# Three-term matmuls on one core: the output products of rounds two to four as seven block products

## The chip, the cores and the metric

The kernel runs on one core of a Trainium2 chip. The core has a matrix engine (PE in the profile, with its weight loads shown apart as PEld), a vector engine (DVE), a scalar engine (ACT), a general engine (POOL) and a queue engine (SP) that issues most transfers. The metric is device time in microseconds for one execution; the median of several runs counts.

## The reference

Attention with a sigmoid in place of the softmax, then a gated MLP with a spatial mixing over the sequence. Eight batches, 12 heads of 64, 448 tokens, model width 768, 1024 hidden columns of which one half (u) is gated by the other (v). All inputs are float32.

```python
scores = scale * (q @ k.T) - log(S)          # per batch and head, S = 448
x = sigmoid(scores) @ v                      # (B, S, 768)
h = relu(x @ w_in)                           # w_in 768 x 1024
u, v = h[..., :512], h[..., 512:]
v_n = (v - mean(v)) / sqrt(var(v) + 1e-6)
v_s = einsum('ts,bsd->btd', w_spatial, v_n) + b_spatial
out = (u * v_s) @ w_out                      # w_out 512 x 768
```

## The kernel before

**Rounds.** The eight batches go in four rounds of two (`m` = 0 to 3 in the code, rounds one to four in the text). A round has these stages, which PE runs one after the other: attention (scores `psc`, sigmoid on ACT, value products `pav`), the v half of the hidden layer (`pv`, with its normalisation), the spatial products (`pg`), the u half (`pu` in round one, `ua` and `ub` in the others), and the output products `po`.

**Three terms.** A float32 factor is kept as a high part and a low part, and a product is three matmuls: high by high, low by high, high by low (`TERMS`). So each operand that is made on the chip costs a rounding copy (its high part, `high` or a CAST, mostly on ACT) and a subtraction (its low part, on DVE).

**Output.** `output(b, es)` makes two of the six 128-wide pieces of one batch's output: for each piece 4 parts of the hidden dimension by 3 terms, 12 matmuls of 448 columns. Six pieces and two batches make 144 matmuls a round. One ACT copy takes two pieces to SBUF and one transfer of 448 KB stores them. The last call of the kernel drains each piece by itself.

**The u half in seven products.** In rounds two to four, `gated_by_blocks` already makes a 2 by 2 block product with seven block products instead of eight (the sums of x's blocks come from `x_sums`, those of the weight's blocks from `weight_sums`, which were made once, in round one's output and at the start of round two, and written to the DRAM tile `w7_u`). The seven blocks of 768 KB are loaded again in each round, four ahead and three while the products run. The results are collected in PSUM and in three SBUF tiles r1, r2, r3 by ACT copies and DVE adds, and `settle` multiplies them into the gates and splits the result for the output products.

**What sets the order.** `in_program_order` keeps every engine's instructions in the order in which the code writes them. An engine takes its instructions strictly in that order, so one that waits holds all behind it on its engine. `jobs` is a list of generators, and `spare(n)` writes their next n steps at the place where it stands: that is how side work for DVE and ACT is woven into a stage. Transfers are issued on SP's queue in written order, those for the next round by `start_loads` and `ahead`.

**PSUM.** `banks(name)` hands out one of four PSUM tiles of two banks each, in turn. A matmul that writes such a tile waits for the instructions that read it before.

Of the kernel before, what the change touches and what calls it, by code (L numbers as in the profile page):

```python
# [14 lines left out]
P = 128  # L15
# [20 lines left out]
def attn_gmlp_kernel(  # L36
# [58 lines left out]
    w_out_s = const.tile([P, NFC * DM // 512, 2, 512], F32R, name="w_out_s")  # L95
# [56 lines left out]
    def weight_steps():  # L152
# [26 lines left out]
        def parts(n):  # L179
            dst, i = steps[n][2:]  # L180
            if dst is None:
                return tuple(w_u[0][:, a, i * F : (i + 1) * F] for a in range(2))
            return dst[:, i, 0], dst[:, i, 1]
# [23 lines left out]

        def begin(n):
# [8 lines left out]
        def middle(n, l, low, a):  # L217
            join(l, low, a)
            nc.scalar.copy(parts(n)[0], l.bitcast(F32))
            return l.bitcast(F32)  # L220
# [197 lines left out]
    def half_of(w, o, k, n):  # L418

        block, col = divmod((o // 2 * n + k) * 2 + o % 2, 4)  # L420
        return w[:, block, :, col * P : (col + 1) * P]
# [20 lines left out]
    def block(pos):  # L442
        flat = w_u[0].rearrange("p a c -> p (a c)")
        at = pos % SLOTS_U * 2 * BLOCK
        return flat[:, at : at + 2 * BLOCK].rearrange("p (a c) -> p a c", a=2)

    def load_block(pos):
        nc.sync.dma_start(block(pos).bitcast(F32), w7_u[pos])

    def weight_sums():  # L450
# [3 lines left out]
        names = ("11", "12", "21", "22")  # L454

        def plain(name, a):
            at = names.index(name) * BLOCK
            return w_u[0][:, a, at : at + BLOCK].bitcast(F32)

# [11 lines left out]
        for i, name in enumerate(names):  # L471
            if name in ORDER:
                at = i * BLOCK
                nc.sync.dma_start(w7_u[ORDER.index(name)], w_u[0][:, :, at : at + BLOCK].bitcast(F32))
        nc.vector.tensor_add(t0, plain("21", 0), plain("21", 1))
        yield True
        nc.vector.tensor_add(t1, plain("22", 0), plain("22", 1))
# [4 lines left out]
        nc.vector.tensor_sub(t0, plain("11", 0), t0)  # L482
        yield True
        nc.vector.tensor_add(t0, t0, plain("11", 1))
# [5 lines left out]
        nc.vector.tensor_sub(t1, t1, plain("11", 0))  # L490
        yield True
        nc.vector.tensor_sub(t1, t1, plain("11", 1))
# [8 lines left out]
        nc.vector.tensor_sub(t1, plain("12", 0), t1)  # L501
        yield True
        nc.vector.tensor_add(t1, t1, plain("12", 1))
# [245 lines left out]
    def settle(b, fcs, g, pu):  # L749

        for at, by in pu if isinstance(pu, list) else [(g, pu)]:
            nc.vector.scalar_tensor_tensor(at, by, 0.0, at, op0=ALU.max, op1=ALU.mult)
        if b % 2:
            gs = [slots["tile"][:, fcs[0] + a, :, :S] for a in range(2)]
        elif b > 1 and not fcs[0]:
            gs = [slots["tile"][:, 4 + a, :, :S] for a in range(2)]
# [7 lines left out]

    def gated_by_blocks(m):

        b0, b1 = 2 * m, 2 * m + 1
        x = {
            name: [
                x_s[:, :, k * KH + ks, j * S : (j + 1) * S] for ks in range(KH)  # L770
# [3 lines left out]
        x |= {name: sums[name] for name in ("t2", "t3", "t4")}  # L774
        r1, r2, r3 = sums.pop("r")

        def products(ps, pos, mv, begins, then=None):
            w = block(pos)
            ops = [(a, ks, c) for ks in range(KH) for a, c in TERMS]
            for i in range(2):  # L780
                for n, (a, ks, c) in enumerate(ops):
                    col = (ks * 2 + i) * P
                    nc.tensor.matmul(  # L783
                        ps[i],
                        w[:, a, col : col + P],
                        x[mv][ks][:, c],
# [410 lines left out]
```

## Time and profile before

| | us |
|---|---|
| Median of 3 runs | 652.48 (651.89 to 652.49) |
| The profiled execution, its own time | 652.91 |
| Its span, first to last instruction | 651.1 |
| PE busy in the span | 646.2 (99%) |
| DVE busy | 399.3 (61%) |
| ACT busy | 311.4 (48%) |
| One round's output products (round two) | 28.80 |
| One round's block products of the u half (round two) | 25.21 |

The profile's chain is followed back from the last instruction: each piece of it ended last before the next could start. Where PE holds nearly all of that chain, a microsecond saved on PE shortens the kernel and one saved elsewhere does not, until another engine makes PE wait. Starts in the rows are microseconds from the start of the span.

### The profile page before, as it was taken

How to read it: one execution, taken by the hardware profiler on the slowest of the kernel's cores; microseconds unless marked ns; L12 is line 12 of the kernel's file. 1: busy time of each engine (PE TensorE's matmuls, PEld its weight loads, DVE VectorE, ACT ScalarE, POOL GpSimd, SP SyncE). 2: the span in 40 equal slices, each digit the busy share in tenths (PEclk: the TensorE clock that was granted, in tenths of full speed). 3: DMA queues.
4: the chain of work that ended last, by engine and by line, in shares of the span. 5: the costliest groups of instructions: out<-in, count | busy, mean ns of one | idle time of the engine just before them, and what ended most of it. 6: DMA issues, size and time to landing. Idle time of an engine off the chain costs nothing.

```text
span 651.1 us, 10058 instructions
## 1 busy us (share of the span) xinstructions
PE 646.2 (99%) x4208; PEld 501.1 (77%) x4208; DVE 399.3 (61%) x561; ACT 311.4 (48%) x377; POOL 28.3 (4%) x63
## 2 busy tenths in 40 slices
PE   9999999999999999999999999999999999999997
PEld 3645789999855678999976558899996665889997
DVE  4989789949555486836155638773516763777320
ACT  5987322323677736222277764522218774541221
POOL 0000010000000001000000001200000000220000
PEclk9999999999999999999999999999999999999999
DMA  8755113465773000047655100004944510001213
GB/s 298 253 185 184 39 59 97 144 219 209 291 292 104 27 1 1 1 145 261 218 172 172 58 2 1 2 5 143 334 172 145 172 58 1 2 1 54 92 57 113
DMA packets 25117, 77.85 MB, mean 120 GB/s; under 512 B 2416, under 2 KB 8944, under 8 KB 25072
## 3 DMA queue, kind: packets, MB, share of 16 engines
q1 hardware_dynamic: 24784, 76.98, 34.1%
q8 instruction: 33, 0.54, 0.3%
q10 hardware_dynamic: 288, 0.23, 0.1%
q14 instruction: 12, 0.10, 0.1%
HBM read 60.69 MB, written 16.52 MB: 119 GB/s over the span
## 4 chain that ended last, share of the span: by engine, by line
PE 99%; ACT 0%; DVE 0%; issue 0%
PE po L407 18%; PE pv L407 18%; PE pav L938 15%; PE psc L325 14%; PE pg L707 10%; PE ua L783 7%; PE pav L374 5%; PE ub L783 5%; PE pu L407 4%; PE psc L307 3%; PE pg L682 1%; PE warm L416 0%; ACT osb L846 0%; DVE ats L412 0%; DVE bias_s L104 0%
## 5 line engine op out<-in xcount | busy, mean ns | idle before, releaser
L407 PE MATMUL pv<-w_g_s,x_s 128*128 128x512 f32 x504 | 115.4, 390 | 0.0
L407 PEld LDWEIGHTS pv<-w_g_s,x_s 128*128 128x128 f32 x504 | 94.3, 188 | 22.3 <-issue 2.1
L289 ACT ACTIVATE ats<-psc,bias_s 128x896 f32<-128x896 f32 x102 | 95.3, 1007 | 20.3 <-PE pav L938 13.6
L325 PEld LDWEIGHTS psc<-qks 64*128 64x128 f32 x840 | 78.1, 185 | 15.2 <-issue 4.9
L325 PE MATMUL psc<-qks 64*128 64x448 f32 x840 | 89.2, 366 | 0.0
L407 PE MATMUL po<-mlp,w_out_s 128*128 128x448 f32 x396 | 82.8, 362 | 0.0
L407 PEld LDWEIGHTS po<-mlp,w_out_s 128*128 128x128 f32 x396 | 74.2, 187 | 5.0
L938 PE MATMUL pav<-ats,v 64*64 64x448 f32 x720 | 76.0, 539 | 0.0
L707 PE MATMUL pg<-w_sp_s,mlp 128*128 128x448 f32 x320 | 65.8, 363 | 0.0
L707 PEld LDWEIGHTS pg<-w_sp_s,mlp 128*128 128x128 f32 x320 | 59.7, 187 | 5.4 <-issue 1.2
L938 PEld LDWEIGHTS pav<-ats,v 64*64 64x64 f32 x720 | 28.3, 132 | 37.4 <-issue 26.6
L851 ACT COPY osb<-po 128x896 f32<-128x896 f32 x23 | 20.9, 908 | 65.2 <-PE po L407 62.0
L123 DVE TENSOR_TENSOR x_s<-pav,x_s 128x896 fp32r<-128x896 f32 x16 | 17.4, 1091 | 50.9 <-ACT x_s L122 50.9
L275 DVE TENSOR_TENSOR qks<-raw,qks 128x848 fp32r<-128x848 f32 x46 | 47.4, 1039 | 1.0
L407 PE MATMUL po<-gs,w_out_s 128*128 128x448 f32 x180 | 39.3, 362 | 0.0
L407 PEld LDWEIGHTS po<-gs,w_out_s 128*128 128x128 f32 x180 | 33.7, 187 | 2.3
L268 DVE CAST qks<-raw 128x848 fp32r<-128x848 f32 x38 | 22.7, 597 | 19.5 <-PE po L407 13.1
L653 DVE SCALAR_TENSOR_TENSOR mlp<-rv,rstd,mlp 128x512 fp32r<-128x512 f32 (+1 forms) x32 | 23.5, 750 | 17.4 <-ACT mlp L648 16.9
L783 PE MATMUL ub<-x_s,w_u_s 128*128 128x448 f32 x162 | 33.9, 362 | 0.0
L938 PE MATMUL pav<-at,v 64*64 64x448 f32 x216 | 31.9, 536 | 0.0
L783 PEld LDWEIGHTS ub<-x_s,w_u_s 128*128 128x128 f32 x162 | 30.4, 187 | 2.0
L910 DVE COPY wval_s<-psc 128x896 f32<-128x896 f32 x9 | 9.8, 1091 | 35.8 <-PE psc L325 35.8
(121 smaller groups left out, 794.1 us busy)
## 6 DMA issues: line engine op xcount, KB each, us to landing
raw<-qk_dram SPq DMA_DIRECT2D x47, 456.0 KB, 5.4
w_u_s<-w_u SPq DMA_DIRECT2D x21, 768.0 KB, 6.0
v<-v_dram SPq DMA_DIRECT2D x24, 448.0 KB, 3.4
out_dram<-osb SPq DMA_DIRECT2D x23, 448.0 KB, 2.6
wraw<-w_in_dram SPq DMA_DIRECT2D x12, 512.0 KB, 4.8
wraw<-w_out_dram SPq DMA_DIRECT2D x6, 512.0 KB, 3.8
w_u<-x_s SPq DMA_DIRECT2D x4, 768.0 KB, 3.6
w_u<-w_u_s SPq DMA_DIRECT2D x3, 768.0 KB, 5.6
```

The source lines that it names most:

```text
L268: (nc.vector.tensor_copy if b > 1 or halfway else nc.scalar.copy)(s[:, 0], raw)
L275: nc.vector.tensor_sub(s[:, 1], loaded[b, hp][:, HALF:], s[:, 0].bitcast(F32))
L289: nc.scalar.activation(at, src, AF.Sigmoid, bias=bias_s, scale=QK)
L307: nc.tensor.matmul(psc[odd * HALF : (odd + 1) * HALF, j, :S], raw[rows, :HALF], raw[rows, HALF + Q :], start=True, stop=True,)
L325: nc.tensor.matmul(psc[:, j, :S], st[rows, k : k + P], mv[rows, Q:PART], start=i == 0, stop=i == len(ops) - 1,)
L374: nc.tensor.matmul(pav[heads, odd, :S], vt[rows, t, heads], at[rows, j], start=start, stop=t == NFULL,)
L407: nc.tensor.matmul(ps, st, mv, start=i == 0, stop=i == len(ops) - 1)
L653: nc.vector.scalar_tensor_tensor(lo, rv[rows, i], rstd[rows, i : i + 1], hi.bitcast(F32), op0=ALU.mult, op1=ALU.subtract,)
L707: nc.tensor.matmul(pg[:, i, :S], st, mv, start=n == 0 and not ended, stop=n == len(ops) - 1 and ended,)
L783: nc.tensor.matmul(ps[i], w[:, a, col : col + P], x[mv][ks][:, c], start=begins and n == 0, stop=n == len(ops) - 1, skip_group_check=True,)
L851: nc.scalar.copy(osb, po[:, :, :S])
L938: ins = nc.tensor.matmul(pavs[pair][heads, i % 2, :S], vt[rows, t if t == NFULL else t + i % 2 * (NFULL + 1), heads], at[rows, j], start=i ...
```

## The change

In rounds two to four the output of two batches is made as a 2 by 2 block product too. With the blocks of the hidden activations g11, g21 (batch one, low and high half of the hidden columns) and g12, g22 (batch two), sums t1 to t4 of them are made, and `output_by_blocks` runs seven block products of 3 pieces by 2 parts by 3 terms, 18 matmuls of 448 columns each: 126 matmuls a round instead of 144. `by_blocks` is the loop that both the u half and the output now use, with one list of products (`PRODUCTS`: which moving block, and which of the accumulators X, W, Y it goes to). For the output, X is the first bank and W and Y are the second bank of three PSUM tiles `o_m_0` to `o_m_2`. `then(pos, i)` is called behind each piece i of product number pos and writes the copies, adds and stores.

The order of the products in the u half changes: the gates are now multiplied in as r1, r3, the X accumulator and r2 come, and the sums of the gated blocks are made there (`high`, `low`). Five steps that are left (`rest`) are woven into the first two products of the output by `spare(1)`.

The seven blocks of w_out: w_out_s is laid out by blocks, three plain blocks are stored at the start of round two, and the sums are made in round two's attention by `output_weight_sums` (14 yields), woven in by `spare`: one step in the first group of two head pairs, five in the second, eight in the third. At the start of `pv` in rounds two to four, four blocks for u and four for the output are loaded (768 KB each), the other three of each while the products run. The transfers for the next attention that stood ahead of the output are in part moved into it, and its first splits too (`between`, behind the product t3). The output leaves as stores of 224 KB.

```diff
-    w_out_s = const.tile([P, NFC * DM // 512, 2, 512], F32R, name="w_out_s")
+    w_out_s = const.tile([P, 2, NFC * DM], F32R, name="w_out_s")
...
+    def half_of(e, fc):
+
+        at = (((e % 2 * 2 + fc // 2) * NCC // 2 + e // 2) * 2 + fc % 2) * P
+        return w_out_s[:, :, at : at + P]
...
-    ORDER = ("11", "12", "s2", "s1", "s3", "22", "s4")
-    SLOTS_U = 4
-    w7_u = dram.tile([NB, P, 2, BLOCK], F32, name="w7_u")
+    ORDER = ("11", "12", "s2", "s3", "s1", "s4", "22")
+    NAMES = ("11", "12", "21", "22")
+    HELD = 4
...
+    def block(flat, pos):
+        at = pos % HELD * 2 * BLOCK
+        return flat()[:, at : at + 2 * BLOCK].rearrange("p (a c) -> p a c", a=2)
+
+    def load_block(flat, pos):
+        w7 = w7_u if flat is flat_u else w7_out
+        nc.sync.dma_start(block(flat, pos).bitcast(F32), w7[pos])
...
+    def keep_plain(w7, w):
+        for name in NAMES:
+            if name in ORDER:
+                at = NAMES.index(name) * BLOCK
+                nc.sync.dma_start(w7[ORDER.index(name)], w[:, :, at : at + BLOCK].bitcast(F32))
+
+    def output_weight_sums(stage):
...
+        def add(i, a, b, op=ALU.add):
+            nc.vector.tensor_tensor(low(i), a, b, op=op)
...
+        def finish(i, name):
+            nc.vector.tensor_sub(low(i).bitcast(F32R), low(i), high(i).bitcast(F32))
+            nc.sync.dma_start(w7_out[ORDER.index(name)], stage[:, i])
+
+        add(0, part("21", 0), part("21", 1))
+        yield True
+        add(0, low(0), part("22", 0))
+        yield True
+        add(0, low(0), part("22", 1))
+        nc.scalar.copy(high(0), low(0))
+        yield True
+        add(1, low(0), part("11", 0), ALU.subtract)
+        yield True
+        add(1, low(1), part("11", 1), ALU.subtract)
+        nc.scalar.copy(high(1), low(1))
+        yield True
+        finish(0, "s1")
+        yield True
...
+        finish(2, "s3")
+        yield True
+        finish(3, "s4")
+        yield True
...
+    PRODUCTS = (("11", X), ("21", W), ("t2", X), ("t3", Y), ("t1", X), ("22", X), ("t4", Y))
+    def by_blocks(flat, stationary, moving, nk, ps, then):
+
+        started = set()
+        for pos, (mv, to) in enumerate(PRODUCTS):
+            w = block(flat, pos)
+            ops = [(a, k, c) for k in range(nk) for a, c in TERMS]
+            for i, out_ps in enumerate(ps[to]):
+                for n, (a, k, c) in enumerate(ops):
+                    nc.tensor.matmul(
+                        out_ps,
+                        stationary(w, i, k)[:, a],
+                        moving[mv][k][c],
+                        start=(to, i) not in started and n == 0,
+                        stop=n == len(ops) - 1,
+                        skip_group_check=True,
+                    )
+                started.add((to, i))
+                then(pos, i)
+            if pos + HELD < NB:
+                load_block(flat, pos + HELD)
...
+        flat = slots["tile"].rearrange("p n a s -> p (n a s)")
+
+        def in_big(n):
+            at = n * 4 * S
+            t = flat[:, at : at + 4 * S].rearrange("p (a i s) -> p a i s", a=2, i=2)
...
+        homes = {
+            "11": in_big(0), "22": in_big(1), "t1": in_big(2), "t2": in_big(3),
+            "21": in_x(0), "t3": in_x(1), "t4": in_x(2),
+        }
+        hid.update({name: [[h[a][:, k] for a in range(2)] for k in range(2)] for name, h in homes.items()})
...
+        def gate(g, by, i=slice(0, 2)):
+            nc.vector.scalar_tensor_tensor(g[:, i], by, 0.0, g[:, i], op0=ALU.max, op1=ALU.mult)
+
+        def high(name, src, i=slice(0, 2)):
+            nc.scalar.copy(homes[name][0][:, i], src[:, i])
+
+        def low(name, src, i=slice(0, 2)):
+            hi, lo = homes[name]
+            nc.vector.tensor_sub(lo[:, i], src[:, i], hi[:, i].bitcast(F32))
+        def rest():
+            low("t2", g22)
+            yield True
+            nc.vector.tensor_sub(g21, g21, g22)
+            high("t4", g21)
+            yield True
+            low("t3", g12)
+            yield True
+            low("t1", g11)
+            yield True
+            low("t4", g21)
+            yield True
+
+        def then(pos, i):
+            if mv == "11":
+                nc.scalar.copy(r1[:, i], px[i])
+            elif mv == "21":
+                nc.vector.tensor_add(r1[:, i], pw[i], r1[:, i])
+                if i:
+                    gate(g11, r1)
+                    high("11", g11)
+                    low("11", g11)
+            elif mv == "t2":
+                nc.scalar.copy(r2[:, i], px[i])
+            elif mv == "t1":
+                nc.scalar.copy(r3[:, i], px[i])
+                nc.vector.tensor_add(r3[:, i], py[i], r3[:, i])
+                if i:
+                    gate(g22, r3)
+                    high("22", g22)
+                    low("22", g22)
+            elif mv == "22":
+                gate(g12, px[i], i)
+                if i:
+                    nc.vector.tensor_sub(g11, g12, g11)
+                    high("t1", g11)
+                    nc.vector.tensor_sub(g12, g22, g12)
+                    high("t3", g12)
+            elif mv == "t4":
+                nc.vector.tensor_add(r2[:, i], py[i], r2[:, i])
+                gate(g21, r2[:, i], i)
+                high("21", g21, i)
+                if not i:
+                    nc.vector.tensor_sub(g22, g22, g11)
+                    high("t2", g22)
+                else:
+                    low("21", g21, 0)
+                    low("21", g21, 1)
+
+        by_blocks(
+            flat_u,
+            lambda w, i, k: w[:, :, (k * 2 + i) * P : (k * 2 + i + 1) * P],
+            x,
+            KH,
+            {X: px, W: pw, Y: py},
+            then,
+        )
+        jobs.append(rest())
...
+    def output_by_blocks(m, final, between):
+
+        b0, b1 = 2 * m, 2 * m + 1
+        n = NCC // 2
+        tiles = [banks(f"o_{m}_{i}") for i in range(n)]
+        px, py = ([ps[:, a, :S] for ps in tiles] for a in range(2))
+        spare_u = sums.pop("r")[2]
...
+        r1 = [spare_u[:, 0], spare_u[:, 1], in_wval(2)]
...
+            else:
+                nc.sync.dma_start(out[b, e], src)
+        def then(pos, i):
+            mv = PRODUCTS[pos][0]
+            if mv == "11":
+                spare(1)
+                nc.scalar.copy(r1[i], px[i])
+            elif mv == "21":
+                if not i:
+                    spare(1)
+                nc.vector.tensor_add(r1[i], py[i], r1[i])
+                leave(b0, i, 0, r1[i])
+                spare(1)
+                if i == n - 1:
+                    spare(99)
+                    pieces("r3", 0)
+                    pieces("c12", 1)
+                    pieces("r2", 2)
+            elif mv == "t2":
+                nc.scalar.copy(later["r2"][i], px[i])
+            elif mv == "t3":
+                if i == n - 1:
+                    between()
+            elif mv == "t1":
+                r3 = later["r3"][i]
+                nc.scalar.copy(r3, px[i])
+                nc.vector.tensor_add(r3, py[i], r3)
+                leave(b1, i, 1, r3)
+            elif mv == "22":
+                nc.scalar.copy(later["c12"][i], px[i])
+                leave(b1, i, 0, later["c12"][i])
+            elif mv == "t4":
+                r2 = later["r2"][i]
+                nc.vector.tensor_add(r2, py[i], r2)
+                leave(b0, i, 1, r2)
...
+        if m < 2:
+            ahead(value_loads, n)
         ahead(attention_loads, n + 2)
+        if m < 2:
+            more_loads(m)
+
+    def more_loads(m):
+        n = m * 2 * NHP
+        if m > 1:
+            ahead(value_loads, n)
         ahead(attention_loads, n + 3)
         if m:
             ahead(value_loads, n + 2)
...
+                spare(8 if n + 4 == end else 3 if n > first else 0)
                 value_steps(1, two[2:3])
                 if n + 4 == end:
                     leave(1, value_steps(1, two[3:]))
                 value_steps(0, [(NFULL, NFULL)])
                 split_values(pavs[0], *units[n])
+                if n + 4 < end:
+                    spare(2 if n > first else 1)
...
+        if m == 1:
+            stage = const.tile([P, 4, 2, BLOCK], F32, tag="w_u", name="stage")
+            keep_plain(w7_out, w_out_s)
+            jobs.append(output_weight_sums(stage))
         attention(m)
         slots_of_mlp(m)
...
+            spare(99)
+            if m == 1:
+                w_u.append(const.tile([P, 2, NCC * F], F32R, tag="w_u", name="w_u_7"))
+            for flat in (flat_u, flat_out):
+                for pos in range(HELD):
+                    load_block(flat, pos)
...
+        def next_splits():
+            if more:
+                for n in range(3):
+                    attention_splits(*units[(m + 1) * 2 * NHP + n])
+
         if m:
             biased(b1, pairs[1])
             spare(99)
             gated_by_blocks(m)
             start_loads(m + 1)
...
-            jobs.append(weight_sums())
+
+            def between():
+                more_loads(m + 1)
+                next_splits()
+
+            output_by_blocks(m, not more, between)
+            continue
```

On PE in round two, the first instructions of the output products. In the kernel before (o_ and po_ are PSUM tiles, mlp, gs and x_s hold the gated activations), the fifth and later matmuls wait for two more split results:

```order
L407 MATMUL po_2_0_2584<-mlp_1_2053,w_out_s_67 128x448 [waits DVE_49]
L407 MATMUL po_2_0_2584<-mlp_1_2053,w_out_s_67 128x448 x5
L407 MATMUL po_2_0_2584<-gs_2_2_2541,w_out_s_67 128x448 [waits Activation_49]
L407 MATMUL po_2_0_2584<-gs_2_2_2541,w_out_s_67 128x448
L407 MATMUL po_2_0_2584<-gs_2_2_2541,w_out_s_67 128x448 [waits DVE_49]
L407 MATMUL po_2_0_2584<-gs_2_2_2541,w_out_s_67 128x448 x3
L407 MATMUL po_2_0_2584<-mlp_1_2053,w_out_s_67 128x448 x6
```

On PE in the changed kernel, round two's output from its second block product (moving x_s, g21) to the start of the third (moving mlp, t2):

```order
L845 MATMUL o_1_0_2611<-x_s_70,w_out_s_67 128x448 [waits DMAHW5_49,Activation_49]
L845 MATMUL o_1_0_2611<-x_s_70,w_out_s_67 128x448
L845 MATMUL o_1_0_2611<-x_s_70,w_out_s_67 128x448 [waits DVE_49]
L845 MATMUL o_1_0_2611<-x_s_70,w_out_s_67 128x448 x2
L845 MATMUL o_1_0_2611<-x_s_70,w_out_s_67 128x448 [waits DVE_49]
L845 MATMUL o_1_1_2612<-x_s_70,w_out_s_67 128x448 [waits Activation_49]
L845 MATMUL o_1_1_2612<-x_s_70,w_out_s_67 128x448 x5
L845 MATMUL o_1_2_2613<-x_s_70,w_out_s_67 128x448 [waits Activation_49]
L845 MATMUL o_1_2_2613<-x_s_70,w_out_s_67 128x448 x5
L845 MATMUL o_1_0_2611<-mlp_1_2076,w_out_s_67 128x448 [waits DMAHW6_49,DVE_49]
L845 MATMUL o_1_0_2611<-mlp_1_2076,w_out_s_67 128x448 x5
L845 MATMUL o_1_1_2612<-mlp_1_2076,w_out_s_67 128x448 [waits DVE_49]
```

Each piece of the second product now starts with a wait for ACT, and the pieces of the third with a wait for DVE.

On ACT in the same place, the end of round two's block products and the start of its output. Before:

```order
L122 CAST mlp_1_2053<-wval_s_74 128x2x448 [waits DVE_49]
L122 CAST gs_2_2_2541<-g_2_2_2354 128x896 [waits DVE_49]
L122 CAST mlp_1_2053<-g_3_0_2380 128x2x448 [waits DVE_49]
L851 COPY osb_2_0_2583<-po_2_0_2584 128x2x448 [waits PE_49,Activation_49]
L851 COPY osb_2_2_2611<-po_2_2_2612 128x2x448 [waits PE_49,Activation_49]
```

After (wval_s holds g22, g_2_0 g11, g_3_0 g12, g_2_2 g21, and ur and wval_s the r1 pieces of the output):

```order
L901 CAST mlp_1_2076<-wval_s_74 128x896 [waits DVE_49]
L901 CAST mlp_1_2076<-g_2_0_2356 128x896 [waits DVE_49]
L901 CAST x_s_70<-g_3_0_2412 128x2x448 [waits DVE_49]
L901 CAST x_s_70<-g_2_2_2386 128x448 [waits DVE_49]
L901 CAST mlp_1_2076<-wval_s_74 128x896 [waits DVE_49]
L901 CAST x_s_70<-g_2_2_2386 128x448 [waits DVE_49]
L998 COPY ur_1_2_2362<-o_1_0_2611 128x448 [waits PE_49]
L901 CAST x_s_70<-g_2_2_2386 128x2x448 [waits DVE_49]
L998 COPY ur_1_2_2362<-o_1_1_2612 128x448 [waits PE_49]
L998 COPY wval_s_74<-o_1_2_2613 128x448 [waits PE_49]
```

Between the drains of the first and the second output piece there now stands the rounding copy of t4 (x_s<-g_2_2, 128x2x448), which waits for DVE.

On ACT in round two's attention, the second group. Before:

```order
L122 CAST x_s_70<-pav_16_0_1795 128x2x448 [waits DMAHW3_49,DMAHW1_49,PE_49]
L289 ACTIVATE at_3_2_3_1853<-psc_3_2_3_1854,bias_s_75 128x2x448 [waits PE_49]
L1023 COPY ats_1_1459<-pav_16_1_1796 128x896 [waits PE_49,Activation_49]
L289 ACTIVATE at_3_4_3_1876<-psc_3_4_3_1877,bias_s_75 128x2x448 [waits PE_49,Activation_49]
L289 ACTIVATE ats_1_1459<-psc_3_2_1_1891,bias_s_75 128x896 [waits PE_49]
```

After:

```order
L503 CAST stage_1456<-stage_1456 128x768 [waits DMAHW3_49,DMAHW1_49,DVE_49]
L122 CAST x_s_70<-pav_16_0_1797 128x2x448 [waits DMAHW3_49,DMAHW1_49,PE_49]
L508 CAST stage_1456<-stage_1456 128x768 [waits DVE_49]
L300 ACTIVATE at_3_2_3_1863<-psc_3_2_3_1864,bias_s_75 128x2x448 [waits PE_49]
L1235 COPY ats_1_1460<-pav_16_1_1798 128x896 [waits PE_49,Activation_49]
L300 ACTIVATE at_3_4_3_1886<-psc_3_4_3_1887,bias_s_75 128x2x448 [waits PE_49,Activation_49]
```

The two rounding copies of w_out's sums (L503, L508) stand ahead of the copy of `pav` and of the short sigmoid, and wait for DVE.

## Rows read from the trace of the kernel before

**Rows 1.** The page: granted clock in 40 slices, and the chain that ended last

```profile
PEclk9999999999999999999999999999999999999999
...
PE 99%; ACT 0%; DVE 0%; issue 0%
```

**Rows 2.** The chain in order of time: start us, us, engine, tile, line, count

```profile
1.23 2.74 PE warm L416 x6
3.97 3.59 PE psc L325 x16
...
229.24 28.80 PE pv L407 x126
...
275.27 3.60 PE ua L783 x18
...
300.48 28.80 PE po L407 x144
```

**Rows 3.** Windows of round two's block products and output, engines' busy us

```profile
core 0: us, PE busy (x) PEld busy (x) DVE busy (x) ACT busy (x) POOL busy (x), PEclk, DMA share, GB/s
300.48:329.28 28.80, 28.80 (x148) 26.72 (x151) 8.42 (x11) 5.49 (x6) 0.00 (x0) 1.00 0.66 240
275.27:300.48 25.21, 25.21 (x128) 23.63 (x127) 11.91 (x16) 6.39 (x10) 0.00 (x0) 1.00 0.43 147
```

**Rows 4.** ACT's timeline in round two's block products: start us, us, [idle before <-releaser]

```profile
286.11 0.53 ACT L797 COPY ur<-ua 128x448 f32<-128x448 f32 x1 [0.37 <-PE ua L783]
...
295.66 0.94 ACT L122 CAST mlp<-wval_s 128x896 fp32r<-128x896 f32 x1 [1.82 <-DVE wval_s L752]
```

**Rows 5.** DVE's timeline in round two's block products, last part

```profile
293.88 0.62 DVE L800 TENSOR_TENSOR ur<-ub,ur 128x448 f32<-128x448 f32 x1 [1.18 <-ACT ur L797]
294.54 1.09 DVE L752 SCALAR_TENSOR_TENSOR wval_s<-ur,wval_s 128x896 f32<-128x896 f32 x1
296.64 1.09 DVE L123 TENSOR_TENSOR mlp<-wval_s,mlp 128x896 fp32r<-128x896 f32 x1 [1.01 <-ACT mlp L122]
297.64 1.15 DVE L752 SCALAR_TENSOR_TENSOR g<-ua,g 128x448 f32<-128x448 f32 x2
```

**Rows 6.** The page's costliest groups: the output's weight loads, the attention's splits; busy, mean ns

```profile
L407 PEld LDWEIGHTS po<-mlp,w_out_s 128*128 128x128 f32 x396 | 74.2, 187 | 5.0
...
L275 DVE TENSOR_TENSOR qks<-raw,qks 128x848 fp32r<-128x848 f32 x46 | 47.4, 1039 | 1.0
...
L268 DVE CAST qks<-raw 128x848 fp32r<-128x848 f32 x38 | 22.7, 597 | 19.5 <-PE po L407 13.1
```

**Rows 7.** DVE's timeline, round one's weight sums and round two's attention

```profile
153.09 0.96 DVE L484 TENSOR_TENSOR wval_s<-wval_s,w_u_s 128x768 f32<-128x768 f32 x1
...
207.59 1.09 DVE L123 TENSOR_TENSOR x_s<-pav,x_s 128x896 fp32r<-128x896 f32 x1 [3.45 <-ACT x_s L122]
...
227.97 1.09 DVE L123 TENSOR_TENSOR x_s<-pav,x_s 128x896 fp32r<-128x896 f32 x1 [8.99 <-ACT x_s L122]
```

**Rows 8.** ACT's timeline, round one's weight sums and round two's attention

```profile
152.15 0.84 ACT L480 CAST x_s<-wval_s 128x768 fp32r<-128x768 f32 x1 [3.94 <-DVE wval_s L479]
...
208.15 1.01 ACT L289 ACTIVATE at<-psc,bias_s 128x896 f32<-128x896 f32 x1 [0.60 <-PE psc L307]
...
210.75 0.91 ACT L1023 COPY ats<-pav 128x896 f32<-128x896 f32 x1 [1.58 <-PE pav L938]
```

**Rows 9.** PE's timeline, the scores of the third group of that attention

```profile
211.02 7.49 PE L325 MATMUL psc<-qks 64*128 64x448 f32 x72
```

**Rows 10.** The page's DMA issues: count, KB each, median us from issue to landing

```profile
w_u_s<-w_u SPq DMA_DIRECT2D x21, 768.0 KB, 6.0
...
out_dram<-osb SPq DMA_DIRECT2D x23, 448.0 KB, 2.6
```

**Rows 11.** ACT's timeline at the end of the kernel

```profile
647.50 0.53 ACT L846 COPY osb<-po 128x448 f32<-128x448 f32 x1 [1.82 <-PE po L407]
```

More of the change, by code (lines that the diff above doesn't have):

```diff
@@ L218, in middle @@
             join(l, low, a)
-            nc.scalar.copy(parts(n)[0], l.bitcast(F32))
-            return l.bitcast(F32)
+            l = shaped(n, l.bitcast(F32))
+            nc.scalar.copy(parts(n)[0], l)
+            return l
         begun, joined = {}, {}
@@ L749, in settle @@
     def settle(b, fcs, g, pu):
-        for at, by in pu if isinstance(pu, list) else [(g, pu)]:
-            nc.vector.scalar_tensor_tensor(at, by, 0.0, at, op0=ALU.max, op1=ALU.mult)
+        nc.vector.scalar_tensor_tensor(g, pu, 0.0, g, op0=ALU.max, op1=ALU.mult)
         if b % 2:
             gs = [slots["tile"][:, fcs[0] + a, :, :S] for a in range(2)]
-        elif b > 1 and not fcs[0]:
-            gs = [slots["tile"][:, 4 + a, :, :S] for a in range(2)]
         else:
@@ L773, in gated_by_blocks @@
         }
[L774 to L786, printed above, removed]
-                        start=begins and n == 0,
-                        stop=n == len(ops) - 1,
-                        skip_group_check=True,
-                    )
-                if then:
-                    then(i)
-            if pos + SLOTS_U < NB:
-                load_block(pos + SLOTS_U)
@@ L821, in gated_by_blocks @@
-        products(pz, 6, "22", False, added_to(r2, pz))
-        settle(b1, pairs[0], gates.pop((b1, pairs[0])), r2)
-    def output(b, es, final=False):
-        osb = work.tile([P, 2, 512], F32, tag="tmp", name=f"osb_{b}_{es[0]}", bufs=3)[:, :, :S]
-        if final:
-            pos = [banks(f"po_{b}_{e}")[:, 0, :S] for e in es]
-        else:
-            po = banks(f"po_{b}_{es[0]}")
-            pos = [po[:, i, :S] for i in range(2)]
+        x |= {
+            name: [[sums[name][ks][:, a] for a in range(2)] for ks in range(KH)]
+            for name in ("t2", "t3", "t4")
+        }
@@ new lines, in gated_by_blocks @@
+        r1, r2, r3 = sums["r"]
+        px = [banks(f"ux_{m}_{i}")[:, 0, :S] for i in range(2)]
+        both = [banks(f"uy_{m}_{i}") for i in range(2)]
+        pw, py = ([ps[:, n, :S] for ps in both] for n in range(2))
+        g11, g21, g12, g22 = (
+            gates.pop(at) for at in ((b0, lo_fc), (b0, hi_fc), (b1, lo_fc), (b1, hi_fc))
+        )
+        flat = slots["tile"].rearrange("p n a s -> p (n a s)")
+        def in_big(n):
+            at = n * 4 * S
+            t = flat[:, at : at + 4 * S].rearrange("p (a i s) -> p a i s", a=2, i=2)
+            return [t[:, a] for a in range(2)]
@@ L1111, in attn_gmlp_kernel @@
             start_loads(m + 1)
[L1112 to L1124 removed]
+            def between():
[3 more added lines that the diff above has]
+            continue
+        gated(b0, pairs[0])
+        biased(b1, pairs[1])
+        gated(b0, pairs[1])
+        gated(b1, pairs[0])
+        start_loads(m + 1)
+        output(b0, (0, 1))
+        gated(b1, pairs[1])
+        jobs.append(weight_sums())
         spare(3)
@@ L1129, in attn_gmlp_kernel @@
         spare(3)
-        if more:
-            for n in range(3):
-                attention_splits(*units[(m + 1) * 2 * NHP + n])
+        next_splits()
         output(b1, (0, 1))
@@ L1136, in attn_gmlp_kernel @@
         spare(3)
-        output(b1, (4, 5), final=not more)
+        output(b1, (4, 5))
         spare(8)
-        if not m:
-            for pos in range(SLOTS_U):
-                load_block(pos)
     in_program_order(tc)
```

149 lines of the change are left out of this document (80 added, 69 removed).

## The prediction

> **What bounds the kernel now.** I read the chain first. It is PE's for 99% [rows 1], so nothing is won by relieving another engine, and all that is cut from PE counts as long as PE is not made to wait. In order of time the output of a round stands in that chain as one unbroken piece of 28.80 us, and the block products of the u half ahead of it in pieces of 3.60 us for 18 matmuls [rows 2]. Both give 0.200 us a matmul of 448 columns at a granted clock of 1.00, the 2.4 GHz level. The windows then tell how much room the other engines have: DVE is busy 8.42 us of the 28.80 us of output and 11.91 us of the 25.21 us of block products, ACT 5.49 and 6.39 us [rows 3]. On the mean that is much room. What matters is whether there is room at the seam between the two stages, where the sums of the gated blocks have to be made. That needs the timelines.
>
> Times below are counted from the start of a round's block products, T (275.27 in round two). The output starts at T + 25.2 (300.48 less 275.27).
>
> **PE's work.** 18 matmuls fewer in each of three rounds, 54 x 0.200 = **10.8 us less**. Weight loads stay hidden: PEld has 187 ns for one [rows 6] beside a matmul of 200 ns.
>
> **The seam.** The order on PE shows that in the second block product each piece i waits for ACT, namely for the copy of r1[i], although it writes the other bank of the PSUM tile; the pieces of the third wait for DVE's add of r1[i]. ACT takes in order: the high part of g21 (second half), copy r1[0], high part of t4, copy r1[1], copy r1[2]. The high part of t4 needs g21 - g22 from DVE, which is DVE's last but three step before its first add for the output. So I follow DVE through the end of the block products, with a PSUM add of 448 columns 0.62 us, a gate of 448 columns 0.55 to 0.58 (1.15 for two), a step of 896 columns 1.00 to 1.12 from start to start, an ACT copy of 448 columns 0.53 and of 896 columns 0.94 [rows 4, 5].
>
> The fifth product (t1) gives its pieces at 16.2 and 18.0; with an ACT copy ahead of each, DVE adds r3 at 16.8 and 18.6, gates g22 at 19.3, waits for its high part, makes its low part at 21.4. That wait of 1.0 us is in the kernel before as well [rows 5]. Only then come the gates of g12 (22.4, 22.9), whose products were ready at 19.8 and 21.6, then g12 - g11 and g22 - g12 (23.6, 24.7). The two r2 adds start at 25.7 and 27.9, though PE was done with those pieces at 23.4 and 25.2: **DVE is 2 us behind** when the output starts. Behind the first add come gate and t2's difference (26.3, 26.9), behind the second a gate (28.6 to 29.2). ACT makes g21's high part to 29.7, and so the copy of r1[0], ready on PE at 26.4, runs 29.7 to 30.2. DVE goes on with g21's two low parts (29.1, 29.8), t2's low part (30.3), and g21 - g22 (31.4 to 32.5). ACT makes t4's high part to 33.4 and the copy of r1[1] to 33.9.
>
> PE: the first product takes 25.2 to 28.8. The second could start at 28.8 and starts at 30.24, **1.44 us late**; its second piece would start at 31.44 and starts at 33.97, **another 2.53 us**. The wait sits on the weight load, so that a load of 0.187 us is shown at the worst at one of them [rows 6]. Sum: 4.16 us a round, 12.5 us in three rounds. All 17 steps of this chain have durations from rows; if each is 0.05 us longer it is 5.0 us a round, if each is 0.06 shorter 3.2. Without the 2 us by which DVE is late it would be 1.4, which I take up as a rival.
>
> Behind this seam the waits have room. The third product starts at 36.6; its pieces need r1's adds, which can run at 35.0 to 36.5 (0.62 each behind DVE's low parts of t3, t1 and t4). Blocks five and six of w_out are issued at about 37.6 and 40.1, behind the stores of r1 on the same queue, and needed at 47.2 and 50.8; at 6.0 us for 768 KB [rows 10] they land at 43.6 and 46. The first splits for the next attention, moved to stand behind the product t3, are three pairs of a cast of 0.60 and a subtraction of 1.04 us [rows 6], 4.9 us, in a stage in which DVE had some 20 us idle [rows 3].
>
> **The sums of w_out's blocks.** 14 DVE steps of 768 columns at 0.96 us [rows 7], and four ACT copies at 0.84 [rows 8], once. The first group has one step, and the third has eight beside an idle stretch of DVE of 8.99 us [rows 7] under the scores and values of PE: nothing. In the second group five steps come at DVE's idle 3.45 us [rows 7], that is 204.1 to 207.6. From about 204.1, one of them behind an ACT copy, they take it to 208.8, and the ACT copy of the fifth runs to 209.7 or later; it stands ahead of the short sigmoid, which ran at 208.15 before, and of the copy of `pav`, at 210.75 [rows 8]. ACT has 1.58 us of slack there and is to do 0.84 more and wait. The PSUM tiles of the scores that PE starts at 211.02 [rows 9] come free later by what ACT is late: between 0 and 1.2 us, and I take **0.6 us**, half, as the late sigmoid is itself not first in PE's order. If the steps find room, 0.
>
> **Transfers.** Three plain blocks stored in round two, eight blocks of 768 KB a round at the start of `pv`: one behind the other 8 x 6.0 = 48 us [rows 10]. From 229.24 that is 277 at the worst, the first four of them for u, done by 253 and needed at 275.27; those for the output are needed at 300.48. Hidden. Stores are 12 of 224 KB in place of 6 of 448 KB; the larger ones land in 2.6 us [rows 10], and the smaller end sooner. Round one does not change: the w_out it loads is the same data in another layout.
>
> **The end.** The last piece was drained by an ACT copy of 0.53 us [rows 11]. Now it is a DVE add of 0.62 us and one more hand-over to the queue of ACT, 0.1 us as between engines in the seam: +0.2 (-0.1 to 0.4).
>
> **Sum.** -10.8 + 12.5 + 0.6 + 0.2 = **+2.5 us**. The profiled execution took 652.91, 0.43 above the median; it would come to 655.4, the median to 655.0. With 3.2 and 5.0 us for the seam, 0 and 1.2 for the sums, -0.1 and 0.4 for the end the median is 651.2 to 658.3.
>
> **Rivals.**
>
> *The seam costs little (faster).* The waits on ACT bind only if ACT is late: from the point on at which r1[0] is copied by 28.8 and r1[1] by 30.0 they cost nothing. Then only the two low parts of g21 are late (done at 29.7 and 30.3), which the third and the sixth matmul of the second product need at 29.2 and 29.8: 0.5 to 0.7 us a round, I take 0.7. 652.5 - 10.8 + 2.1 + 0.8 = 644.6. For it: the copies are ready on PE 2.4 us before, and if DVE was not late at the start, the seam would cost 1.4 (646.7). Against it: DVE's sequence is long whatever the one duration is, and to reach 30.0 t4's high part would have to come 3.4 us sooner. A rule would bring the same time: the Trainium skill (PSUM — Partial Sum Buffer, section "PSUM bank collisions raise a hardware error") lets TensorE write one bank while another engine reads a different one, so that a guard by bank would let the second product start without the copies. By that rule the wait is not the chip's need; the program as ordered holds it all the same. Chance 0.14, with cases between 644.6 and 651.
>
> *The clock falls in the waits (much slower).* The one time it comes from idle is the start: six matmuls of 512 columns took 2.74 us, 0.457 each, where the same in `pv` take 28.80 / 126 = 0.229 [rows 2], half the rate, and the 16 score matmuls behind them took 0.224 each. That is 6.3 us at half rate. As much behind the waits of a round would lose 3.2 us: 655.0 + 9.6 = 664.6. Against it: the granted clock reads the upper level in all slices [rows 1], and the waits worked out here are short. The Trainium skill (TensorE: Matmul & The Clock Gate, section "HAM oscillation — how this bites in real kernels") tells of kernels whose TensorE waits again and again for its data and restarts at the lower clock each time; by that rule 664.6 is the time if these waits are long enough for it, and no row here tells. Chance 0.04.
>
> *A block of w_out comes late (slower).* Blocks five and six wait behind the stores of r1 on SP. From the point at which one lands 3.6 us later than 6.0 after issue PE waits; at twice the 6.0 us it is 2.4 us a round: 657.4 with one round, 662 with three. The queue carries 240 GB/s in this stage before [rows 3]. Chance 0.06.
>
> **How the numbers follow.** Forecast 0.76, its own range 651.2 to 658.3, time 655.0. The range of 8 in 10 takes in the milder late blocks and the nearest of the cheap seam: 650.5 to 659.5. Faster or slower counts from 0.2%, 1.3 us, about what a measurement of this kernel can tell. Faster (below 651.2): 0.14 and a little of the forecast's edge, 0.15. Same (651.2 to 653.8): 0.18 of the forecast. Slower: 0.57 of the forecast and 0.10 of the last two rivals, 0.67.
>
> **What would show it.** The output stage 25.2 us of matmuls and about 4 us of waits, 29 to 29.6 us, in the two places named, with ACT's rounding copy of t4 ahead of the copy of r1[1]; PE idle of 12 to 13 us in all; some 0.6 us before the scores of the third group of round two's attention. The forecast is wrong if the second product starts as the first ends, if the waits lie elsewhere, or if the granted clock falls below 1.00.

## The result: slower by 1.2%

The changed kernel takes 660.24 us (659.62 to 661.15, four runs) beside 652.24 for the kernel before (651.89 to 652.49, four runs): a ratio of 1.0124, 95% interval 1.0107 to 1.0142. Forecast were 655.0 us and a range up to 659.5, so the side was right, and the time came out above the range. The profiled execution has a span of 659.3 us (651.1 before) and a mean granted clock of 0.988 (1.000 before).

The page of the changed kernel, its span, busy times, clock in 40 slices and chain, which answers to [rows 1]:

```profile
span 659.3 us, 10184 instructions
...
PE 642.7 (97%) x4154; PEld 495.3 (75%) x4154; DVE 450.5 (68%) x629; ACT 324.9 (49%) x410; POOL 28.8 (4%) x63
...
PEclk9999999999999999998999999999799999999989
...
PE 91%; DVE 6%; ACT 2%; DMA 1%; issue 0%; SPq 0%; DVEq 0%
```

PE is busy 3.5 us less than before, though 10.8 us of matmuls are gone: some matmuls have become slower. Its granted clock drops in the three places where the outputs of rounds two, three and four stand, and DVE and ACT now hold 6% and 2% of the chain, where each held 0% [rows 1]. The chain in order of time shows those pieces, the rows that answer to [rows 2] (start us, us, what; round two):

```profile
229.95 28.79 PE pv L418 x126
...
275.97 3.60 PE ux L845 x18
...
307.39 1.01 DVE g L910
308.43 0.94 ACT x_s L901
309.85 22.11 PE o L845 x102
331.96 1.66 PE psc L318 x16
...
470.87 23.40 PE o L845 x102
...
633.19 22.29 PE o L845 x102
```

Behind the seam, the same 102 matmuls take 22.11, 23.40 and 22.29 us where 102 x 0.200 would be 20.40. So there are two losses, the wait and a slower PE behind it. PE's waits by releaser (us in total, times, longest us), and PE's timeline in rounds two, three and four, which show both:

```profile
PE o L845 <- ACT ur L998: 10.8, 6, 2.2
```

```profile
306.21 1.48 PE L845 MATMUL o<-x_s,w_out_s 128*128 128x448 f32 x6 [1.44 <-ACT ur L998]
309.85 4.11 PE L845 MATMUL o<-x_s,w_out_s 128*128 128x448 f32 x12 [2.15 <-ACT ur L998]
313.79 3.76 PE L845 MATMUL o<-mlp,w_out_s 128*128 128x448 f32 x18
317.39 3.76 PE L845 MATMUL o<-x_s,w_out_s 128*128 128x448 f32 x18
...
470.87 4.85 PE L845 MATMUL o<-x_s,w_out_s 128*128 128x448 f32 x12 [2.15 <-ACT ur L998]
475.52 4.35 PE L845 MATMUL o<-mlp,w_out_s 128*128 128x448 f32 x18
479.71 3.76 PE L845 MATMUL o<-x_s,w_out_s 128*128 128x448 f32 x18
...
633.19 4.26 PE L845 MATMUL o<-x_s,w_out_s 128*128 128x448 f32 x12 [2.15 <-ACT ur L998]
...
640.90 3.76 PE L845 MATMUL o<-x_s,w_out_s 128*128 128x448 f32 x18
```

The windows around them (columns as in [rows 3]) give the clock. In round two it falls in the second wait and is back at the upper level by 313; in round three it stands at the lower level, 0.50, to about 476.8; in round four it falls only behind the wait, which ends at 633.19. Round three's stretch at 0.50, from about 470, is the longest, and it loses most:

```profile
306.20:307.70 1.50, 1.48 (x6) 1.05 (x6) 1.50 (x3) 0.00 (x0) 0.00 (x0) 1.00 0.80 295
307.70:309.80 2.10, 0.00 (x0) 0.00 (x0) 2.10 (x3) 1.37 (x3) 0.00 (x0) 0.93 0.34 135
309.80:311.00 1.20, 1.15 (x3) 1.07 (x4) 1.20 (x3) 0.43 (x1) 0.00 (x0) 0.50 0.00 0
311.00:313.00 2.00, 2.00 (x7) 1.76 (x7) 1.37 (x2) 0.00 (x0) 0.00 (x0) 0.52 0.31 115
...
469.00:471.00 2.00, 0.13 (x1) 0.13 (x1) 2.00 (x3) 1.55 (x3) 0.00 (x0) 0.74 0.17 71
471.00:473.00 2.00, 2.00 (x6) 1.78 (x7) 1.96 (x3) 0.26 (x1) 0.00 (x0) 0.50 0.11 38
473.00:475.00 2.00, 2.00 (x7) 1.79 (x6) 0.62 (x1) 0.00 (x0) 0.00 (x0) 0.50 0.24 85
475.00:477.00 2.00, 2.00 (x7) 1.77 (x7) 1.14 (x3) 0.00 (x0) 0.00 (x0) 0.56 0.31 115
...
631.00:633.10 2.10, 0.04 (x1) 0.00 (x0) 2.10 (x3) 1.33 (x3) 0.00 (x0) 1.00 0.21 85
633.10:635.00 1.90, 1.81 (x6) 1.65 (x7) 1.90 (x3) 0.47 (x2) 0.00 (x0) 0.68 0.00 0
635.00:637.00 2.00, 2.00 (x7) 1.74 (x7) 0.90 (x2) 0.00 (x0) 0.00 (x0) 0.50 0.35 130
```

**Where the 8 us come from.** Stage by stage, start of the next less start of this, after less before: the start of the kernel to round two's attention +0.1; that attention +0.6 (59.72 less 59.13); the three outputs +2.0, +3.3 and +2.2 (30.79, 32.07 and 30.97 beside 28.80); the end +0.2. What the lower clock takes is read from the starts: from the second piece to the fourth product, 30 matmuls take 7.54, 8.84 and 7.71 us where 30 x 0.200 is 6.00. That is 1.5, 2.8 and 1.7 us, 6.1 in all. An output then has 25.20 of matmuls at full rate, 3.59 of shown waits, about 0.5 by which PE is late beyond them when it stops and starts again, and this.

### The profile page after: what moved, and what is told of

It is laid out like the page before. It is cut to its first block, busy times and chain, and to the rows that moved or that the text cites. A ratio compares the mean times of both kernels' runs of the same rounds, so it can differ in the third digit from the quotient of the medians.

```text
span 659.3 us, 10184 instructions
## 1 busy us (share of the span) xinstructions
PE 642.7 (97%) x4154; PEld 495.3 (75%) x4154; DVE 450.5 (68%) x629; ACT 324.9 (49%) x410; POOL 28.8 (4%) x63
## 4 chain that ended last, share of the span: by engine, by line
PE 91%; DVE 6%; ACT 2%; DMA 1%; issue 0%; SPq 0%; DVEq 0%
PE pv L418 17%; PE pav L1147 15%; PE psc L336 13%; PE o L845 10%; PE pg L779 10%; PE pav L385 5%; PE ux L845 5%; PE pu L418 4%; PE po L418 4%; PE uy L845 3%; PE psc L318 3%; DVE g L898 1%; DVE mlp L905 1%; DMA raw<-qk_dram 1%; ACT x_s L901 1%; PE pg L754 1%
## 5 line engine op out<-in xcount | busy, mean ns | idle before, releaser
L845 PE MATMUL o<-x_s,w_out_s 128*128 128x448 f32 x162 | 40.2, 405 | 10.8 <-ACT ur L998 10.8
L845 PEld LDWEIGHTS o<-x_s,w_out_s 128*128 128x128 f32 x162 | 34.0, 213 | 15.7 <-ACT ur L998 13.0
L845 PE MATMUL o<-mlp,w_out_s 128*128 128x448 f32 x216 | 45.3, 366 | 0.0
L845 PEld LDWEIGHTS o<-mlp,w_out_s 128*128 128x128 f32 x216 | 41.3, 191 | 2.8
L845 PE MATMUL ux<-x_s,w_u 128*128 128x448 f32 x162 | 33.4, 362 | 0.0
L845 PEld LDWEIGHTS ux<-x_s,w_u 128*128 128x128 f32 x162 | 30.4, 188 | 2.0
L418 PE MATMUL pu<-x_s,w_u_s 128*128 128x448 f32 x144 | 29.1, 362 | 0.0
L418 PEld LDWEIGHTS pu<-x_s,w_u_s 128*128 128x128 f32 x144 | 27.0, 188 | 1.8
L385 PE MATMUL pav<-ats,v 128*64 128x448 f32 (+1 forms) x144 | 27.1, 545 | 0.0
## 6 DMA issues: line engine op xcount, KB each, us to landing
w_out_s<-w_out SPq DMA_DIRECT2D x21, 768.0 KB, 11.3
```

The source lines that it names most:

```text
L385: nc.tensor.matmul(pav[heads, odd, :S], vt[rows, t, heads], at[rows, j], start=start, stop=t == NFULL,)
L418: nc.tensor.matmul(ps, st, mv, start=i == 0, stop=i == len(ops) - 1)
L845: nc.tensor.matmul(out_ps, stationary(w, i, k)[:, a], moving[mv][k][c], start=(to, i) not in started and n == 0, stop=n == len(ops) - 1, s ...
```

## The experiments

**The copies of r1 first.** ACT's copies no longer stand behind t4's high part; DVE's order is unchanged.

```diff
             if mv == "11":
-                spare(1)
                 nc.scalar.copy(r1[i], px[i])
+                if i == n - 1:
+                    spare(3)
```

> The changed kernel with the three ACT copies of r1 written ahead of the rounding copy of t4, DVE's order unchanged. The second wait of each output (2.15 us shown, 2.44 with the reload) should be gone, the first (1.44) stay. Theory 1, the lower granted clock follows from the waits and needs the longer one: 660.2 less 3 x 2.44 less 6.5 of lost clock = 646.4, granted clock 1.00. Theory 2, any of these waits brings the clock down: 652.9, clock still about 0.99. Rival, the clock falls for another reason in this stage (DVE, transfers): also 652.9.

Measured: 652.1 us (ratio 0.9996, 0.9987 to 1.0006), granted clock 0.999. The second wait is gone and the clock stays up, as theory 1 had it, but the time is 5.7 us over its 646.4. PE's timeline in round two, and DVE's, show why:

```profile
305.78 3.88 PE L845 MATMUL o<-x_s,w_out_s 128*128 128x448 f32 x18 [1.44 <-ACT ur L997]
310.55 4.21 PE L845 MATMUL o<-mlp,w_out_s 128*128 128x448 f32 x18 [0.89 <-DVE ur L1003]
```

```profile
306.87 1.08 DVE L910 TENSOR_TENSOR g<-g,wval_s 128x896 f32<-128x896 f32 x1
307.87 1.08 DVE L905 TENSOR_TENSOR x_s<-g,x_s 128x896 fp32r<-128x896 f32 x1
308.87 1.08 DVE L905 TENSOR_TENSOR mlp<-g,mlp 128x896 fp32r<-128x896 f32 x1
309.88 0.62 DVE L1003 TENSOR_TENSOR ur<-o,ur 128x448 f32<-128x448 f32 x1
310.41 1.08 DVE L905 TENSOR_TENSOR x_s<-g,x_s 128x896 fp32r<-128x896 f32 x1
311.41 0.62 DVE L1003 TENSOR_TENSOR ur<-o,ur 128x448 f32<-128x448 f32 x1
```

DVE makes g21 - g22 and the low parts of t2, t3 and t1 ahead of r1's adds, so with the second wait gone the third product waits for the add of r1[0] (0.89 us) and its second piece for that of r1[1] (it cannot start before 312.0). That is what was late next. In the changed kernel the longer wait had covered it. Theory 2 named the same time for another reason, and the clock row speaks against it.

**Both waits away.** The last gate, g21's parts and t2's sum are written into the output behind the copies of r1, and t2's low part and the rest behind the adds of r1. `left[0]` writes the last r2 add, its gate and the high and low parts of g21, `left[1]` g22 - g11 and t2's high part; they are taken out of the last product of the u half.

```diff
             if mv == "11":
-                spare(1)
                 nc.scalar.copy(r1[i], px[i])
+                if not i:
+                    left[0]()
+                elif i == n - 1:
+                    left[1]()
             elif mv == "21":
-                if not i:
-                    spare(1)
                 nc.vector.tensor_add(r1[i], py[i], r1[i])
                 leave(b0, i, 0, r1[i])
-                spare(1)
+                if i == 1:
+                    spare(1)
```

> The changed kernel with the last gate, g21's parts and t2's sum written into the output behind the copies of r1: ACT takes copy r1[0], high part of g21's second half, copies r1[1] and r1[2], then t2's high part; DVE adds r2, gates and makes g21's low parts before g22 - g11. By the rows both waits should go (r1[0] by 28.0 for 28.8, r1[1] by 29.3 for 30.0, g21's second low part by 29.4 for 29.8). Theory 1 and 2 (the clock falls with the waits): granted clock 1.00 and 652.2 - 10.8 + 0.9 = 642.3. Rival, the clock falls for another reason: clock still 0.99 and about 648.8.

Measured: 643.80 us, ratio **0.9868** (0.9853 to 0.9883), granted clock 0.999. The same 378 matmuls, transfers and sums as in the changed kernel, 16.4 us faster, in another order. Of PE's waits this is left:

```profile
PE o L845 <- DVE mlp L905: 0.6, 3, 0.2
```

So 8.4 of the 10.8 us that the seven products save come through, and neither the transfers nor the larger work of DVE in this stage bring the clock down where PE does not wait: the rival is out.

**The second product's result in a tile of its own.**

```diff
+        apart = banks(f"w_{m}")
+        pw = [apart[:, 0, :S], apart[:, 1, :S], py[2]]
...
-                nc.vector.tensor_add(r1[i], py[i], r1[i])
+                nc.vector.tensor_add(r1[i], pw[i], r1[i])
...
-            {X: px, W: py, Y: py},
+            {X: px, W: pw, Y: py},
```

> The changed kernel with the second product's first two pieces in the fourth PSUM tile, the third in its old place. If the wait belongs to the PSUM tile (as the order has it), pieces one and two no longer wait for the copies of r1, only 0.5 to 0.7 us for g21's low part, and the third piece waits for the copy of r1[2] at 34.46: about 2.6 us, so a seam of 3.2 instead of 3.9. Time 660.2 - 2 = 658 with the clock still falling behind the 2.6 us. If the second product waits for something else (its moving block, its weights), the waits stay where they are: 660.2.

Measured: 665.23 us (ratio 1.0196, 1.0181 to 1.0211), clock 0.984. The expectation missed the time, and by the rule that it meant to test: pieces one and two now share a tile, and the second waits for the reader of the first.

```profile
304.79 1.19 PE L845 MATMUL w<-x_s,w_out_s 128*128 128x448 f32 x4 [0.51 <-DVE x_s L905]
310.05 2.61 PE L845 MATMUL w<-x_s,w_out_s 128*128 128x448 f32 x6 [4.07 <-DVE ur L1004]
312.46 2.44 PE L845 MATMUL o<-x_s,w_out_s 128*128 128x448 f32 x6
...
318.41 3.76 PE L845 MATMUL o<-x_s,w_out_s 128*128 128x448 f32 x18
```

Piece one starts at once and waits only 0.51 us for g21's low part. Piece two, which writes the other bank of `w`, waits 4.07 us for DVE's add that reads the first. The wait follows the tile and not the bank. Behind it the 30 matmuls lose 2.4 us to the lower clock in this round, 2.8 and 3.0 in the next two.

**One wait of three lengths.** On the kernel without waits, idle ACT copies of 896 columns ahead of the copy of r1[1] make one wait in each output. What they write is read by nobody. The edit is shown with three; the other two have two and four.

```diff
             if mv == "11":
+                if i == 1:
+                    for _ in range(3):
+                        nc.scalar.copy(x_s[:, 0, 0:2, S:], x_s[:, 1, 0:2, S:].bitcast(F32))
                 nc.scalar.copy(r1[i], px[i])
```

> As e4_one_wait with two idle copies in place of three: one wait of about 1.1 us in each output. If a wait of this length leaves the clock alone, as the first one of e1 (1.44 us, then 18 matmuls in 3.88 us) did: 643.8 + 3 x 1.2 = 647.4 and granted clock 1.00. If each wait costs clock in proportion, some 0.5 us a round more, 649.

> The kernel of e2_no_wait with three idle copies of 896 columns on ACT ahead of the copy of r1[1]: one wait of PE of about 2.1 us in each output (r1[1] at 32.1, wanted at 30.0), nothing ahead of it. 642.3 + 6.3 = 648.6 if such a wait leaves the clock alone, up to 6.5 us more (655) if it brings it down as in the changed kernel.

> As e4_one_wait with four idle copies: one wait of about 3.0 us in each output. 643.8 + 3 x 3.1 = 653.1 by the wait alone; with the clock falling in every round by 1.7 to 3 us as behind the waits of the changed kernel, 658 to 662, granted clock near 0.985.

Measured, one run each, so that the times have no interval and the readings rest on the traces: 647.46 us at clock 1.000, 652.9 at 0.994, 657.72 at 0.992. The matmuls behind the wait, PE's timeline of the shorter one (round two), the middle one (rounds two, three and four) and the longer one (round two), a fence each:

```profile
306.22 2.67 PE L845 MATMUL o<-x_s,w_out_s 128*128 128x448 f32 x12 [1.05 <-ACT ur L1006]
```

```profile
307.44 2.67 PE L845 MATMUL o<-x_s,w_out_s 128*128 128x448 f32 x12 [2.02 <-ACT ur L1006]
...
465.66 4.27 PE L845 MATMUL o<-x_s,w_out_s 128*128 128x448 f32 x12 [2.02 <-ACT ur L1006]
...
473.38 3.76 PE L845 MATMUL o<-x_s,w_out_s 128*128 128x448 f32 x18
...
625.02 3.60 PE L845 MATMUL o<-x_s,w_out_s 128*128 128x448 f32 x12 [2.02 <-ACT ur L1006]
...
632.74 3.76 PE L845 MATMUL o<-x_s,w_out_s 128*128 128x448 f32 x18
```

```profile
308.94 4.07 PE L845 MATMUL o<-x_s,w_out_s 128*128 128x448 f32 x12 [2.99 <-ACT ur L1006]
...
316.65 3.76 PE L845 MATMUL o<-x_s,w_out_s 128*128 128x448 f32 x18
```

Behind 1.05 us the matmuls run at full rate in all three rounds. Behind 2.02 us they do in round two and lose 1.7 us in rounds three and four, with the same program (30 matmuls in 7.72 us); behind 2.99 us they lose 1.7 to 1.8 us in each round. The middle one's windows say that it is the clock: 1.00 behind the wait in round two, 0.50 in round three.

```profile
307.40:309.00 1.60, 1.56 (x8) 1.47 (x9) 0.00 (x0) 1.26 (x2) 0.00 (x0) 1.00 0.57 224
...
467.00:469.00 2.00, 2.00 (x7) 1.79 (x6) 0.95 (x2) 0.00 (x0) 0.00 (x0) 0.50 0.03 8
```

So a wait alone, with nothing else changed but idle copies on ACT, brings the clock down. Between these two lengths its price does not grow with the wait: 1.7 us behind 2.02, 1.7 to 1.8 behind 2.99.

**What is left.** Three orders more on the kernel without waits: t2's low part ahead of r1's second add together with an earlier place for a step of w_out's sums; the sums alone; and the first of these with t4's difference and rounding moved behind the copies of r2 as well. The first diff is the sums, the second t2's low part, the third t4.

```diff
-                    spare(2 if n > first else 1)
+                    spare(1 if n > first else 2)
```

```diff
                 leave(b0, i, 0, r1[i])
-                if i == 1:
+                if not i:
                     spare(1)
```

```diff
             low("t2", g22)
             yield True
-            nc.vector.tensor_sub(g21, g21, g22)
-            high("t4", g21)
-            yield True
             low("t3", g12)
             yield True
             low("t1", g11)
             yield True
+            nc.vector.tensor_sub(g21, g21, g22)
+            high("t4", g21)
+            yield True
...
-                    spare(99)
+                    spare(2)
...
                 nc.scalar.copy(later["r2"][i], px[i])
+                if i == n - 1:
+                    spare(99)
```

> The kernel of e2_no_wait with two more moves: t2's low part stands ahead of the second add of r1 (in e2 PE waits 0.2 us for it, with the reload 0.35 to 0.45 us a round), and the steps of w_out's sums go 2, 3 and 1, 8 in the three groups of round two's attention instead of 1, 3 and 2, 8, so that the ACT copy of the fifth step comes 2 us sooner. 643.8 - 1.2 - 0.5 = 642.1. If the sums' place was not what made that attention 0.5 us longer, 642.6.

> The kernel of e2_no_wait with the steps of w_out's sums alone moved (2, 3 and 1, 8 in place of 1, 3 and 2, 8), t2's low part where e2 has it. e5_both made both moves and came out at 644.4 against 643.8. By e5's trace round two's attention is 59.38 us from its first score to pv against 59.63 in e2, so the move should bring 0.25: 643.5. If the move of the sums is what made e5 slower, 644.4.

> The kernel of e5_both with the difference and the rounding copy of t4 moved behind the copies of r2 in the third product (t4 is the last product, needed at 46.8 from the start of the block products). In e5 the fourth product waits 0.23 us (about 0.65 us a round with the reload and a slower start) for the copy of r2[0], which stands behind t4's high part on ACT; that should go. The stage should take 25.2 to 25.3 us, 644.4 - 3 x 0.55 = 642.8. If the fourth product waits for something else, 644.4.

Measured: 644.41 us (ratio 0.9878, 0.9862 to 0.9895), **643.02** (0.9865, 0.985 to 0.988) and 645.22 (0.9896, 0.988 to 0.9913). Moving the sums takes round two's attention to 59.31 us, from 59.63 in the kernel without waits and 59.13 before the change, so their place was part of its cost. Bringing t2's low part forward moves the wait of 0.2 us from the third product to the fourth, which then waits for the copy of r2[0] behind t4's high part; making t4 later in turn sends the sixth product to wait for DVE's r3 adds, which come behind the first splits of the next attention. In e9's rounds two and three:

```profile
PE o L845 <- DVE or L1028: 2.1, 2, 1.3
```

A part of what the first and the third lose is not PE's: from PE's last matmul to the end of the span it is 4.9 us in both, beside 3.8 in the second and in the kernel without waits, and the last store on ACT's queue lands after 3.1 us in the former and 2.0 in the latter. Why is open.

The intervals of 643.0 and 643.8 overlap; which of them is better is not settled. Both beat both kernels.

## Why the prediction was wrong

**Right: PE's work, and the seam to a tenth of a microsecond.** The steps put the second product at T + 30.24 and its second piece at T + 33.97; the trace has 306.21 and 309.85 less 275.97, that is 30.24 and 33.88. The high part of t4 was to end at 33.4 and ends at 33.40. The two waits with stopping and starting came to 4.05 us a round where 4.16 was the term. One bound of the sum is a little off: 17 steps that are 0.06 us shorter give 3.1 us a round and not 3.2, which would put the low end at 651.0 and not 651.2. ACT's copies stand where the order has them, and the first of the rivals, that the seam costs little, is out: [rows 4, 5] carried it.

**Right: the sums (+0.6 for 0.6), the end (+0.2 for 0.2), the transfers.** The sums cost by the way forecast, though in the third group's scores and not before them: there PE's weight loads wait 0.15 us for the copy of `pav` and 0.41 us for the late sigmoid. That the size agrees is luck, as 0.6 was taken as the half of 0 to 1.2. No wait of PE for a block is in the trace. The blocks of w_out take 11.3 us from issue to landing in the median, not 6.0 as the u blocks did in [rows 10]; the cover of 71 us was long enough all the same.

**Wrong: the clock.** The step that failed is that the sum has no term for the clock: every matmul behind the waits stands in it at 0.200 us. That was set aside with the second rival, given 0.04 because the waits "worked out here are short". They were long enough, and the granted clock fell below 1.00, one of the prediction's own signs of being wrong. The lower clock cost 6.1 us, and without it the time would have been 654.1, inside the forecast's own range. Its price per round was put at 3.2 us from the start of the kernel [rows 2], and measured 1.5, 2.8 and 1.7: an upper end. The evidence read as speaking against it, a granted clock at the upper level in every slice [rows 1], was none: PE of the kernel before never waits inside a round, so its rows could not show what a wait does. The rival had to be given the weight of a question that the trace leaves open, and the range, which ended at 659.5, had to reach its 664.6. The Trainium skill (TensorE: Matmul & The Clock Gate, section "HAM oscillation — how this bites in real kernels") tells of a kernel whose TensorE waits for data before every tile and starts each one at the lower clock. The rows agree as to the fall, 0.50 behind the waits in three of three rounds; here, though, it took no endless waiting, but two waits of 1.44 and 2.15 us in an output of 31 us.

**And the rule of the banks.** The Trainium skill (PSUM — Partial Sum Buffer, section "PSUM bank collisions raise a hardware error") asks, in its simple version, only for different banks between TensorE and a reader. No run here took the guard by tile away, so none shows that the chip would do without it. What the runs show is that the program's waits go by the tile, two banks at once (1.44 and 2.15 us in the changed kernel, 4.07 us with the tile apart), so that a layout with two accumulators in the banks of one tile ties a product to the drain of the one ahead of it.

## What to carry to other kernels

Before moving sums and roundings to the seam between two matmul stages, follow the in-order engines through the seam step by step with durations from the trace: that found both waits here before the run, and writing the drains ahead of the roundings and subtractions was worth 16 us. Price a wait of PE of 2 us or more at up to about twice its length, since the granted clock can fall in it or just behind it (waits of 1.05 and 1.44 us left it alone here), and take the trace of a kernel that never waits as no evidence that it won't. When a wait is taken away, look for the one that it covered: here four in a row came up behind ACT's copies of r1 (DVE's adds of r1, t2's low part, the copy of r2, DVE's adds of r3).

## What the runs showed of the hardware

The granted clock fell from 1.00 to 0.50 in waits of PE of 2.0 to 4.1 us, or up to 1.5 us behind their end, in the midst of kernels whose PE was busy 97 to 98% of the span, and the matmuls behind ran at half rate for some microseconds (12 of them in 4.65 us in round three of the changed kernel, 0.388 each beside 0.200). The same wait of 2.02 us in one program brought the clock down in rounds three and four and not in round two; what decides between them is open.
